# Key-value sums of a linear-attention and MLP kernel: two groups of eight token tiles in the place of three groups of six, six and four

## The chip, the cores and the metric

The kernel runs on one core of one Trainium2 chip. The core has five engines that work side by side, each through an instruction list of its own: PE (TensorE, matrix products), DVE (VectorE), ACT (ScalarE), POOL (GpSimd) and SP (SyncE, which here only issues DMAs). They meet through semaphores: an instruction waits until another engine's counter has reached a value, and everything behind it on its own engine waits with it. The metric is the time of one execution on the device, in microseconds; lower is better.

## The reference, cut to what matters

The input is one sequence of 2048 tokens with 448 features, in bf16. After a layernorm, two branches are computed and added to it.

```python
xn = layernorm(x)                                  # x: (1, 2048, 448)
# branch A: 16 heads of 28, linear attention with a softmax feature map
q, k, v = split(xn @ wqkv)                         # per head
phi(t)  = concat(softmax(t @ w_phi), softmax(-t @ w_phi))
kv  = einsum("bhsf,bhsd->bhfd", phi(k), v)         # sum over all 2048 tokens
z   = phi(k).sum(over tokens)
num = phi(q) @ kv;  den = phi(q) @ z + 1e-6
A   = (num / den) @ wo
# branch B: a token-shifting MLP
h   = gelu(layernorm(xn) @ w1);  hs = shift(h) @ w2;  x1 = xn + hs
B   = x1 + gelu(layernorm(x1) @ w3) @ w4           # w3: 448 x 1792, w4: 1792 x 448
out = xn + A + B
```

The change is about `kv` (and `z`, which is computed with it): a sum over all tokens that must be complete before the first `num` can be computed.

## The kernel before, in words

The 2048 tokens are 16 tiles of 128, and four tiles make a token group of 512. One token tile is one block of 128 partitions. All data stays in SBUF; PSUM has eight banks, and each is reused many times.

A recorder (`Recorder`, lines 19 to 222) takes every operation in the order in which the Python code calls it, works out from the bytes that each one reads and writes which waits are needed, and then plays each engine's list. So an engine's order is the order of the calls that use it, and moving a call in the list moves its instructions only against those of the same engine. Because helpers record everything, all matrix products have line 204 in the profile, activations line 212, other element-wise work line 216.

After a first stage (layernorm, v, the w1 products and the start of the feature maps) the order is written out by hand in one list, lines 1055 to 1079, of pairs of a short name and its arguments. The names that matter here:

- `k0(n)`, `k1(n)`, `q0(n)`, `q1(n)`: the two halves of the phi products of token tiles 2n and 2n+1. `k1` and `q1` end with two exponentials on ACT. `kn(n)` (DVE) and `kx(n)` (POOL) normalise phi(k) afterwards.
- `w0(i)`, `w1_(i)`: the two halves of the w2 product of tiles i and i+1; `w1_` ends with two additions on DVE, which read PSUM banks 4 and 5 for i = 12 and 14.
- `K(i)` = `kv_tile`, the key-value sum of token tile i: 16 matrix products of 128 rows by 30 columns over 64 columns, all added up in PSUM bank 6. It reads `vaug` (v, a column of ones) and `phik` (phi(k)).
- `kc` = `kv_turn` and `kb` = `kv_blocks`, one DVE instruction each: the finished sum is transposed out of bank 6, then spread into `kvq`, which the attention products read.
- `a(p)`, `b(p)`: the two halves of w3 pair p, that is of 256 of the 1792 columns for 512 tokens. Pairs 0 to 6 belong to the first token group, 7 to 13 to the second. `a` is 8 products, `b` is 6, and `b` ends with one gelu on ACT that reads two PSUM banks into `h3T`. Even pairs use banks 2 and 3, odd pairs banks 0 and 1, so `a(p)` may start only when the gelu of pair p-2 has read its banks.
- `N(i)` = `num_tile` and `o_T`: the attention of token tile i. 16 products go to banks 6 and 7; DVE reads them with a reciprocal, three multiplications or additions and one more combined operation, then inverts the denominator; POOL divides, a DMA transposes. Every `N` uses the same two banks, so the next one waits for the last of these reads.
- `f(n, k)`: quarter n of the output products of tiles 2k and 2k+1; `f(1, k)` and `f(2, k)` are 28 products each and use w4.
- `AD(i)`, `A(i)`: the second layernorm's application on DVE or POOL; `G(i)`, `T(i)`, `S(i)` are DMAs; `lo(i)` is a layernorm statistic on DVE.

Two functions in the code:

```python
741        def kv_tile(i):
742            for n in range(4):
743                for j in range(4):
744                    h = 8 * (j // 2) + 2 * n + j % 2
745                    R.mm(banks[6][HP * j:HP * j + VP, 64 * n:64 * n + 64], vaug[:, i, VP * h:VP * h + VP],
746                         phik[:, i, 2 * h:2 * h + 2, :].rearrange("p g e -> p (g e)"), i == 0 and n == 0, False)

807            b = 1 - p % 2
808            a = lap_pair([banks[2 * b + k] for k in range(2)],
...
812            def late():
813                a[1]()
814                R.act(h3T[:, g % 2, fc:fc + 2, :], two(2 * b), ACT.Gelu_apprx_tanh)
```

Nearly all other products use the array as two halves of 64 rows, two products at a time, one in each half; `K` uses all 128 rows, with four column strips. Buffers are shared: `h3T` lies over `phik` (pair p overwrites the bytes of token tile p, for p up to 13), and the scratch of `N` and of the output lies over `vaug`. Tile i of the key-value sum must therefore be done before the gelu of pair i writes.

Before, PE's order in the part that is changed is: the end of `q0(7)`; K of tiles 0, 7, 8, 3, 1, 5; `q1(7)`, `w1_(12)`; K of tiles 2, 4, 9, 10, 11, 6; a0 a1 b0 b1; `w0(14)`; a2 a3 b2 b3; `w1_(14)`; a4 a5 b4 b5; K of tiles 15, 14, 13, 12; a6 a7 b6 b7; N1, f(1,0), N0; a9 a8 b9 b8; N3, f(2,0), N2; and so on. DVE has `kc` and `kb` behind `AD(11)`, then the work of N1, `AD(10)`, `AD(9)`, the work of N0, `lo(12)`, the work of N3, `lo(15)`, the work of N2.

Of the kernel before, what the change touches and what calls it, by code (L numbers as in the profile page):

```python
# [224 lines left out]
def bass_parallel_sum__linear_kernel_hedgehog__mixer_s_mlp__prompt_kernel(  # L225
# [17 lines left out]
    with es:  # L243
# [807 lines left out]
        def wo_in(eng="SP"):  # L1051
            load_lap(wo, A_wo, (eng, eng))

        K, G, S, T, kc, kb, W = kv_tile, g_T, store, q_T, kv_turn, kv_blocks, fin_tails
# [4 lines left out]
            (kn, 3), (T, 2), (kx, 3), (w1_, 6), (lo, 2), (lo, 3), (q1, 4), (k0, 5), (sc, 0), (k0, 6), (k1, 5),  # L1059
            (w0, 8), (k1, 6), (kn, 4), (w1_, 8), (A, 0), (T, 5), (q0, 5), (q0, 6), (T, 4), (q1, 5), (AD, 1), (w0, 10),  # L1060
            (T, 7), (A, 3), (k0, 7), (kn, 5), (A, 2), (w1_, 10), (q1, 6), (lo, 7), (w0, 12), (k1, 7), (lo, 4),
            (q0, 7), (lo, 5), (T, 6), (load_w4, 1), (lo, 6), (K, 0), (kx, 4), (K, 7), (K, 8), (K, 3), (kn, 6), (K, 1),
            (G, 0), (G, 1), (K, 5), (q1, 7), (w1_, 12), (kx, 5), (K, 2), (K, 4), (G, 3), (kn, 7), (K, 9), (G, 2),
            (K, 10), (lo, 11), (sc, 4), (A, 7), (lo, 10), (A, 6), (AD, 5), (K, 11), (K, 6), (a, 0), (a, 1), (A, 4),
            (b, 0), (lo, 8), (b, 1), (load_w4, 0, g_tok[:, 3, :]), (lo, 9), (kx, 6), (w0, 14), (kx, 7), (a, 2), (G, 6), (a, 3),
            (b, 2), (sc, 8), (b, 3), (w1_, 14), (a, 4), (a, 5), (b, 4), (G, 7), (G, 5), (b, 5), (G, 4), (lo, 13),
            (K, 15), (K, 14), (K, 13), (K, 12), (T, 12), (AD, 11), (T, 11), (T, 8), (kc,), (kb,), (a, 6), (T, 9),
            (a, 7), (b, 6), (b, 7), (N, 1), (AD, 10), (AD, 9), (G, 10), (f, 1, 0), (N, 0), (a, 9), (a, 8), (G, 9),
            (b, 9), (lo, 12), (b, 8), (N, 3), (lo, 15), (f, 2, 0), (N, 2), (a, 10), (AD, 8), (a, 11), (G, 11),
            (b, 10), (f, 3, 0), (lo, 14), (sc, 12), (b, 11), (G, 8), (f, 4, 0), (AD, 14), (a, 12), (T, 14), (a, 13),  # L1070
            (S, 1), (N, 5), (f, 1, 1), (b, 13), (f, 3, 1), (AD, 15), (T, 10), (N, 4), (b, 12), (T, 13), (T, 15),
# [42 lines left out]
```

## Time and profile before

| what | value |
|---|---|
| three runs | 170.65, 170.97 and 173.65 us, median 170.97 |
| the profiled execution's own time | 171.18 us |
| its span in the profile | 169.4 us |
| busy: PE, DVE, POOL, ACT | 164.9, 109.3, 88.0, 81.9 us |
| granted TensorE clock | 1.00 of full speed |

The span runs from the first instruction's start to the last one's end; 1.8 us of the execution's own time lie outside it. Matrix products overlap, so busy PE says that products are under way and not that PE works at its peak: what counts is from when to when a group of products is started. In a timeline each row has the start, the time from the first start to the last end, engine, line, operation, what is written and read, the shape, and how many instructions were merged; in brackets stands the idle time before it and what ended that. The next row's start tells how long PE really spent on a row. In such rows `K` reads `phik,vaug`, w3 pairs read `gT,w`, `N` reads `kvq`, w2 reads `hT` and `hRT`, and `f(1, k)` and `f(2, k)` read `w,phik`.

### The profile page before, as it was taken

How to read it: one execution, taken by the hardware profiler on the slowest of the kernel's cores; microseconds unless marked ns; L12 is line 12 of the kernel's file. 1: busy time of each engine (PE TensorE's matmuls, PEld its weight loads, DVE VectorE, ACT ScalarE, POOL GpSimd, SP SyncE). 2: the span in 40 equal slices, each digit the busy share in tenths (PEclk: the TensorE clock that was granted, in tenths of full speed). 3: DMA queues.
4: the chain of work that ended last, by engine and by line, in shares of the span. 5: the costliest groups of instructions: out<-in, count | busy, mean ns of one | idle time of the engine just before them, and what ended most of it. 6: DMA issues, size and time to landing. Idle time of an engine off the chain costs nothing.

```text
span 169.4 us, 5409 instructions
## 1 busy us (share of the span) xinstructions
PE 164.9 (97%) x2355; PEld 101.2 (60%) x2355; DVE 109.3 (64%) x248; ACT 81.9 (48%) x112; POOL 88.0 (52%) x119
## 2 busy tenths in 40 slices
PE   8799999999999999999999999999999999999994
PEld 7467778776888875535554555554555555544453
DVE  3689854459999999973998766833753647340031
ACT  4589976769998877455242240424310404024000
POOL 5378990002999999890455274362263342734040
PEclk9999999999999999999999999999999999999999
DMA  5995455599999670959464575753412112113011
GB/s 155 353 209 96 77 95 148 115 275 251 272 164 167 199 96 5 223 115 138 92 67 92 65 151 100 151 122 91 86 40 60 58 31 60 33 31 112 0 54 54
DMA packets 50583, 19.93 MB, mean 118 GB/s; under 512 B 41728, under 2 KB 49856, under 8 KB 50560
## 3 DMA queue, kind: packets, MB, share of 16 engines
q1 hardware_dynamic: 49440, 18.71, 56.1%
q10 hardware_dynamic: 1120, 0.89, 1.7%
q8 instruction: 18, 0.29, 0.8%
q14 instruction: 5, 0.04, 0.1%
HBM read 7.14 MB, written 1.84 MB: 53 GB/s over the span
## 4 chain that ended last, share of the span: by engine, by line
PE 92%; DMA 3%; DVE 2%; POOL 1%; SPq 0%; issue 0%
PE banks L204 91%; DMA xtok<-in_A_x_dram 3%; DVE st L216 1%; PE banks L208 1%; POOL rs L216 1%; SPq L222 0%; DVE mv L216 0%; POOL xn L216 0%; DVE xn L216 0%; DVE vaug L216 0%
## 5 line engine op out<-in xcount | busy, mean ns | idle before, releaser
L212 ACT ACTIVATE phik<-banks 128x1024 bf16<-128x1024 f32 (+1 forms) x44 | 41.2, 988 | 62.4 <-PE banks L204 62.3
L216 DVE TENSOR_TENSOR vaug<-banks,vaug 128x464 f32<-128x464 f32 (+3 forms) x65 | 32.8, 514 | 21.4 <-PE banks L204 19.7
L204 PE MATMUL banks<-gT,w 64*128 64x512 bf16 x392 | 46.5, 376 | 0.1
L204 PE MATMUL banks<-w,phik 64*128 64x448 bf16 (+3 forms) x434 | 45.2, 343 | 0.0
L216 POOL TENSOR_TENSOR xnT<-vaug 128x280 bf16<-128x280 f32 (+1 forms) x32 | 18.2, 589 | 41.9 <-DVE vaug L216 41.9
L739 POOL TENSOR_TENSOR phik<-phik,rks 128x1792 bf16<-128x1792 bf16 x8 | 25.6, 3212 | 17.4 <-DVE rks L216 16.9
L204 PEld LDWEIGHTS banks<-w,phik 64*128 64x128 bf16 (+1 forms) x434 | 22.5, 94 | 19.3 <-issue 0.4
L204 PE MATMUL banks<-wv,xnT 64*128 64x448 bf16 (+2 forms) x222 | 32.2, 346 | 0.0
L204 PEld LDWEIGHTS banks<-gT,w 64*128 64x128 bf16 x392 | 18.5, 94 | 20.1 <-ACT phik L212 1.5
L216 POOL TENSOR_TENSOR vaug<-xn,xtok 128x448 f32<-128x448 bf16 x16 | 16.2, 1031 | 8.8 <-DVE vaug L216 8.8
L204 PEld LDWEIGHTS banks<-wv,xnT 64*128 64x128 bf16 (+1 forms) x222 | 13.9, 94 | 7.9 <-PE banks L204 0.5
L204 PE MATMUL banks<-xnT,w 64*128 64x512 bf16 (+1 forms) x105 | 16.7, 334 | 0.0
L216 DVE TENSOR_REDUCE ksum<-phik 128x64 f32<-128x1792 bf16 x8 | 16.0, 1997 | 0.2 <-ACT phik L212 0.2
L216 DVE RECIPROCAL vaug<-banks 128x16 f32<-128x16 f32 x16 | 4.0, 252 | 18.7 <-PE banks L204 18.7
L204 PE MATMUL banks<-wpk,xnT 64*128 64x448 bf16 x112 | 15.7, 349 | 0.0
L204 PE MATMUL banks<-wpq,xnT 64*128 64x448 bf16 x112 | 15.2, 349 | 0.0
L212 ACT ACTIVATE hi<-banks 128x896 bf16<-128x896 f32 x16 | 14.0, 936 | 2.1 <-PE banks L204 2.1
L204 PE MATMUL banks<-w,hT 64*128 64x448 bf16 x96 | 14.4, 349 | 0.0
L216 POOL TENSOR_TENSOR rs<-mv,mhalf 128x1 f32<-128x1 f32 (+1 forms) x14 | 9.7, 700 | 1.9 <-DVE mv L216 1.9
L204 PEld LDWEIGHTS banks<-wpk,xnT 64*128 64x128 bf16 x112 | 9.2, 94 | 2.0
L216 DVE TENSOR_TENSOR xn<-banks,xn 128x512 bf16<-128x512 f32 (+1 forms) x16 | 8.9, 596 | 2.0 <-PE banks L204 2.0
L216 DVE BATCH_NORM_STATS2 st<-xtok 128x6 f32<-128x448 bf16 x15 | 9.1, 604 | 1.5 <-DMA xtok<-in_A_x_dram 1.5
(68 smaller groups left out, 167.6 us busy)
## 6 DMA issues: line engine op xcount, KB each, us to landing
w<-in_B_w_dram SPq DMA_DIRECT2D x2, 896.0 KB, 5.7
out_dram<-vaug SPq DMA_DIRECT2D x15, 112.0 KB, 1.9
w<-in_B_w_dram SPq DMA_DIRECT2D x2, 784.0 KB, 5.3
xtok<-in_A_x_dram SPq DMA_DIRECT2D x2, 448.0 KB, 6.8
wv<-in_A_wo_dram SPq DMA_DIRECT2D x2, 224.0 KB, 4.1
xtok<-in_A_x_dram SPq DMA_DIRECT2D x3, 112.0 KB, 4.4
xtok<-in_A_x_dram ACTq DMA_DIRECT2D x3, 112.0 KB, 4.6
w<-in_B_w_dram SPq DMA_DIRECT2D x1, 336.0 KB, 3.9
```

The lines of the kernel that those rows point to most:

```text
L204: self.op("PE", lambda e: e.matmul(out, lhsT, rhs, start=start, stop=stop, skip_group_check=True), [out], [lhsT, rhs], tile=self._tile(lhsT))
L208: self.op("PE", lambda e: e.transpose(out, in_, ident), [out], [in_, ident], tile=self._tile(in_))
L212: self.op("ACT", lambda e: e.activation(out, in_, func, **kw), [out], [in_] + aps)
L216: self.op(eng, lambda e: getattr(e, name)(out, *args, **kw), [out], aps)
L739: R.op(pool, lambda e: e.tensor_tensor(ph, ph, wide, op=ALU.mult), [ph], [ph, wide, *after])
```

## The change

Only the order in the list changes. The K of tiles 0 to 7 now stand together, behind `q1(7)` and `w1_(12)`. The K of tiles 8 to 15 stand together, behind a6 a7 b6 b7 (pair 7 is the first of the second token group), followed by `kc` and `kb`. The halves a9 and a8 are moved from behind N0 to ahead of N1.

```diff
-            (q0, 7), (lo, 5), (T, 6), (load_w4, 1), (lo, 6), (K, 0), (kx, 4), (K, 7), (K, 8), (K, 3), (kn, 6), (K, 1),
-            (G, 0), (G, 1), (K, 5), (q1, 7), (w1_, 12), (kx, 5), (K, 2), (K, 4), (G, 3), (kn, 7), (K, 9), (G, 2),
-            (K, 10), (lo, 11), (sc, 4), (A, 7), (lo, 10), (A, 6), (AD, 5), (K, 11), (K, 6), (a, 0), (a, 1), (A, 4),
+            (q0, 7), (lo, 5), (T, 6), (load_w4, 1), (lo, 6), (kx, 4), (kn, 6), (G, 0), (G, 1), (q1, 7), (w1_, 12), (K, 0), (K, 7),
+            (K, 3), (K, 1), (K, 5), (K, 2), (K, 4), (K, 6), (kx, 5), (G, 3), (kn, 7), (G, 2), (lo, 11), (sc, 4), (A, 7),
+            (lo, 10), (A, 6), (AD, 5), (a, 0), (a, 1), (A, 4),
             (b, 0), (lo, 8), (b, 1), (load_w4, 0, g_tok[:, 3, :]), (lo, 9), (kx, 6), (w0, 14), (kx, 7), (a, 2), (G, 6), (a, 3),
             (b, 2), (sc, 8), (b, 3), (w1_, 14), (a, 4), (a, 5), (b, 4), (G, 7), (G, 5), (b, 5), (G, 4), (lo, 13),
-            (K, 15), (K, 14), (K, 13), (K, 12), (T, 12), (AD, 11), (T, 11), (T, 8), (kc,), (kb,), (a, 6), (T, 9),
-            (a, 7), (b, 6), (b, 7), (N, 1), (AD, 10), (AD, 9), (G, 10), (f, 1, 0), (N, 0), (a, 9), (a, 8), (G, 9),
+            (T, 12), (AD, 11), (T, 11), (T, 8), (a, 6), (T, 9),
+            (a, 7), (b, 6), (b, 7), (K, 8), (K, 9), (K, 10), (K, 11), (K, 13), (K, 12), (K, 15), (K, 14), (kc,), (kb,),
+            (a, 9), (a, 8), (N, 1), (AD, 10), (AD, 9), (G, 10), (f, 1, 0), (N, 0), (G, 9),
             (b, 9), (lo, 12), (b, 8), (N, 3), (lo, 15), (f, 2, 0), (N, 2), (a, 10), (AD, 8), (a, 11), (G, 11),
```

The number of instructions and the data that each reads and writes are the same. On every engine other than PE the order of the instructions stays as it was.

## Prediction

> **What bounds the kernel now.** First the page: busy times, and the chain of work that ended last.
>
> ```profile
> span 169.4 us, 5409 instructions
> PE 164.9 (97%) x2355; PEld 101.2 (60%) x2355; DVE 109.3 (64%) x248; ACT 81.9 (48%) x112; POOL 88.0 (52%) x119
> PE 92%; DMA 3%; DVE 2%; POOL 1%; SPq 0%; issue 0%
> ```
>
> PE is busy for 97% of the span and holds 92% of the chain. So time is won only where PE issues sooner, and lost wherever PE must wait. Next the waits of PE's weight loads from 40 us on, which come ahead of each product and so show what PE waits for (total, times, longest):
>
> ```profile
> PEld banks L204 <- ACT phik L212: 1.9, 8, 0.4
> ```
>
> In 130 us the largest entry is 1.9 us, and much of that is hidden behind products still running. There is almost no idle PE to remove; the question is whether the new order keeps PE as full. Now PE's timeline through the changed part.
>
> ```profile
> 61.48 0.98 PE L204 MATMUL banks<-wpq,xnT 64*128 64x448 bf16 x8
> 62.39 1.08 PE L204 MATMUL banks<-phik,vaug 128*30 128x64 bf16 x96
> 63.41 0.74 PE L204 MATMUL banks<-wpq,xnT 64*128 64x448 bf16 x6
> 63.98 0.73 PE L204 MATMUL banks<-w,hT 64*128 64x448 bf16 x6
> 64.64 0.95 PE L204 MATMUL banks<-phik,vaug 128*30 128x64 bf16 x96
> 65.70 3.20 PE L204 MATMUL banks<-gT,w 64*128 64x512 bf16 x28
> 68.72 0.75 PE L204 MATMUL banks<-w,hT 64*128 64x448 bf16 x6
> ...
> 72.50 0.75 PE L204 MATMUL banks<-w,hT 64*128 64x448 bf16 x6
> 73.15 3.25 PE L204 MATMUL banks<-gT,w 64*128 64x512 bf16 x28
> 76.32 0.77 PE L204 MATMUL banks<-phik,vaug 128*30 128x64 bf16 x64
> ...
> 77.03 3.20 PE L204 MATMUL banks<-gT,w 64*128 64x512 bf16 x28
> 80.06 0.38 PE L204 MATMUL banks<-kvq,eqT_lo 64*128 64x60 bf16 x16
> 80.28 2.81 PE L204 MATMUL banks<-w,phik 64*128 64x448 bf16 x28
> 82.93 0.38 PE L204 MATMUL banks<-kvq,eqT_lo 64*128 64x60 bf16 x16
> 83.15 3.18 PE L204 MATMUL banks<-gT,w 64*128 64x512 bf16 x28
> 86.17 0.38 PE L204 MATMUL banks<-kvq,eqT_lo 64*128 64x60 bf16 x16
> 86.39 2.81 PE L204 MATMUL banks<-w,phik 64*128 64x448 bf16 x28
> 89.04 0.38 PE L204 MATMUL banks<-kvq,eqT_lo 64*128 64x60 bf16 x16
> ```
>
> Start to next start gives PE's prices. 28 w3 products take 68.72 - 65.70 = 3.02 us, 0.216 per concurrent pair: 0.86 for an `a`, 0.65 for a `b`. f(1,0) takes 82.93 - 80.28 = 2.65, 0.189 per pair; an N 0.22. A K group of 64 products takes 77.03 - 76.32 = 0.71, of 96 takes 63.41 - 62.39 = 1.02: 9.7 ns per product and about 0.09 beside. Entering: the six products at 63.98 would be followed at 64.55, and K starts at 64.64, 0.09 late (0.15 at 62.39).
>
> Then the two engines that PE may have to wait for: ACT's gelus and the last of its exponentials, and DVE.
>
> ```profile
> 72.07 1.94 ACT L212 ACTIVATE phik<-banks 128x1024 bf16<-128x1024 f32 x2 [1.84 <-PE banks L204]
> 75.79 1.94 ACT L212 ACTIVATE phik<-banks 128x1024 bf16<-128x1024 f32 x2 [1.78 <-PE banks L204]
> 79.62 1.94 ACT L212 ACTIVATE phik<-banks 128x1024 bf16<-128x1024 f32 x2 [1.89 <-PE banks L204]
> ...
> 91.84 1.02 ACT L212 ACTIVATE phik<-banks 128x1024 bf16<-128x1024 f32 x1 [4.17 <-PE banks L204]
> ```
>
> ```profile
> 66.61 1.09 DVE L216 TENSOR_TENSOR xn<-banks,xn 128x512 bf16<-128x512 f32 x2
> ...
> 77.17 0.45 DVE L216 STREAM_TRANSPOSE w<-banks 128x256 f32<-128x256 f32 x1 [0.21 <-PE banks L204]
> 77.66 0.65 DVE L216 TENSOR_TENSOR kvq<-w,pick 128x464 bf16<-128x464 f32 x1
> 80.49 0.26 DVE L216 RECIPROCAL vaug<-banks 128x16 f32<-128x16 f32 x1 [2.18 <-PE banks L204]
> ...
> 82.34 0.18 DVE L216 SCALAR_TENSOR_TENSOR vaug<-banks,vaug 128x16 f32<-128x16 f32 x1
> ...
> 82.72 0.98 DVE L216 TENSOR_SCALAR g_tok<-xn,mv,rs 128x512 bf16<-128x512 bf16 x2
> 83.63 0.24 DVE L216 RECIPROCAL vaug<-banks 128x16 f32<-128x16 f32 x1
> ...
> 85.47 0.18 DVE L216 SCALAR_TENSOR_TENSOR vaug<-banks,vaug 128x16 f32<-128x16 f32 x1
> ...
> 88.45 0.18 DVE L216 SCALAR_TENSOR_TENSOR vaug<-banks,vaug 128x16 f32<-128x16 f32 x1
> ```
>
> **The change, step by step**, in the clock of this trace. No instruction is added or removed; what changes is which work covers which wait.
>
> *1. First group, a gain that is mostly a loan.* q0(7) is done issuing at 61.48 + 4 x 0.19 = 62.24. q1(7) and w1_(12) now follow at once, 64.55 - 63.41 = 1.14 us. With 0.09 to enter, K starts at 63.47. Eight tiles are 128 products; the second group of before, 96 products up to a0, took 65.70 - 64.64 = 1.06 (a0 has several waits to pass), so 1.06 + 32 x 0.0097 = 1.37 and a0 starts at 64.84, 0.86 earlier. Of this, four tiles' worth (64 products, 0.62) comes back in the second group. The rest, 0.24, is the gap of one group fewer. Bounds for what a group costs in gaps: nothing, if the neighbours' starts hide it, and 0.15 + 0.13 = 0.28 with the widest entry and a0's slower exit (1.06 - 96 x 0.0097); I take the 0.24 that the rows add up to. Up to b5 all of PE then runs 0.86 earlier. Cover: w0(14) would start at 67.86 and needs the additions of w1_(12) out of banks 4 and 5, which end on DVE at 66.61 + 1.09 = 67.70: 0.16 us of slack, so no wait, and not much more could be gained here.
>
> [...]
>
> *2. A new wait ahead of a6.* In before, the four K tiles stand between b5 and a6. Now a6 follows b5. a6 writes banks 2 and 3, which the gelu of pair 4 must have read. In before that gelu runs from 75.79 for 1.02 and b5's last slot ends at 76.32 - 0.09 = 76.23. Shifted by 0.86: PE is free at 75.37, the gelu ends at 75.95. A semaphore takes about 0.05 us. The row at 72.07 shows the same wait at its edge: that gelu ends at 73.09 and a4 starts at 73.15, although w1_(14), the row at 72.50, lies between. So a6 starts at 76.00: **0.63 us of wait**. Behind it on PE stand a7, b6, b7 and the K group; ACT waits for b6. a7 needs the second gelu of that row, done at 75.79 + 1.94 - 0.86 = 76.87, and starts at 76.92, 0.06 late.
>
> *3. K8 to K15, then a9, a8, N1.* a7 from 76.92, b6 77.78, b7 78.43, its last slot ends at 79.08. K enters at 79.17; 128 products by the rows are 0.71 + 64 x 0.0097 = 1.33, so PE is free at 80.50. a9 needs the gelu of pair 7. In before b6 ends at 77.03 + 2 x 0.86 + 0.65 = 79.40 and its gelu starts at 79.62, 0.22 later; now it starts at 78.65, and the two end 1.94 later at 80.59. a9 starts at 80.64 (**0.14 wait**), a8 at 81.50, N1 at 82.36. The sum itself is no bound: the last K starts at 80.41; in before from there (77.03 - 0.09 = 76.94) to the end of `kb` (77.66 + 0.65 = 78.31) is 1.37, so `kvq` is ready at 81.78, with a9 and a8 as its cover. Without that cover N1 would lose 1.3 us. N1 comes 2.30 later than its 80.06, with 1.72 of a9 and a8 already done: a net loss of 0.58.
>
> *4. The work that covered N0's reads is gone.* Between N0 and N3 stood a9, a8, b9, b8 (3.02 us); now only b9 and b8 (1.30). N3 writes banks 6 and 7, so it waits for DVE's last read for N0, the combined operation at 85.47, done at 85.65, which is 5.59 us behind N1's start at 80.06. That DVE stretch is full (the reads for N1 end at 82.52, the denominator, then AD(10) and AD(9) for 0.98, the reads for N0 from 83.63 without idle time), its order is unchanged, and it starts with N1. So N3 can start 5.64 after N1, at 88.00. PE would be there after 0.22 + 2.65 + 0.22 + 1.30 = 4.39, at 86.75: **1.25 us of wait**, the largest term. f(2,0) and N2 stand behind it, and DVE's work for N3. The same once more for N2: the reads for N3 end at 88.63, 8.57 behind N1, hence N2 at 82.36 + 8.62 = 90.98, while PE is ready at 88.00 + 2.87 = 90.87: 0.11 more. From N2 on PE has the order of before; N2 was at 89.04, so all comes **1.94 us later**.
>
> Sum: a6 0.63, a7 0.06, a9 0.14, N3 1.25, N2 0.11 are 2.19; less 0.24 is 1.95, which closes with N2's own 1.94. Against the profiled execution (span 169.4, own time 171.18) that makes 173.1; it lies 0.2 above the median of the runs, 170.97, from which I forecast 170.97 + 1.94 = **172.9 us**. The measurement can tell about 2% from no change (3.4 us), so this counts as no change, on the slow side.
>
> **Rivals.**
>
> *No net wait* (the new gaps fall on cover, only the saved group counts): 170.97 - 0.24 = 170.7. It needs gelus that end 0.6 us sooner and DVE 1.25 us ahead. For it speaks that ACT idles before each pair of gelus (1.8 us); against it, that this idle time ends with PE, so ACT can't start sooner. 10%.
>
> *Only the front counts*: the N3 wait is absorbed because DVE, idle for 2.18 us ahead of N1, has more in hand than I see. Then 0.58 remains: 171.5. Against: `AD(10)` and `AD(9)` stand behind N1's work in DVE's list. 12%.
>
> *The granted clock falls* in the longer wait. Point: if 1.25 us of idle PE near N3 lowers the clock to half for the next f(2,0), that costs its 2.65 us again: 170.97 + 1.94 + 2.65 = 175.6, clearly slower. This row has PE idle for 1.08 of 4 us at the start (the third number from its end is the granted clock):
>
> ```profile
> 4.00:8.00 4.00, 2.92 (x61) 1.70 (x57) 2.32 (x7) 2.48 (x8) 1.33 (x2) 1.00 1.08 351
> ```
>
> The clock there is 1.00, so I give this 6%. [...]
>
> **How the numbers follow.** Forecast 72%, by its bounds 172.2 to 173.6: 0.2 below for the group's upper bound, some 0.5 either way for what the runs differ among themselves. The range 171.0 to 173.8 takes in that case and the second rival, and leaves out the first and the third with a rest for small waits that I have not seen. Over 2% faster (below 167.6) none of the cases gives: 2%. Over 2% slower (above 174.4): the clock, and a rest, 8%. Within: 90%.
>
> **What would show it.** In the changed trace: two K groups of 128 products; a0 about 0.9 us earlier; PE idle ahead of a6, released by ACT, 0.6 us; a short one ahead of a9; N1 at about 82.4; N3 about 5.6 us behind N1, with over 1 us idle released by DVE; from N2 on the same rows 1.9 us later. I would be wrong if DVE ran the reads for N0 sooner behind N1, if something else held N1, for example the transposed queries, or if f(3,0) now waited for the attention of N0.

## The result, and the profile after

The changed kernel is slower by 1.4%: the ratio to the kernel before is 1.0142, 95% interval 1.0114 to 1.0170, that is 2.4 us on 171.0 (1.9 to 2.9). Three of its six executions took 173.24 to 173.72 us; the other three fell into a slower state and took 176.49 to 176.59, which lifts the plain median to 175.11, outside the forecast range, and the ratio leaves such executions out on both sides.

The page after:

```profile
span 171.6 us, 5409 instructions
PE 165.3 (96%) x2355; PEld 101.2 (59%) x2355; DVE 109.2 (64%) x248; ACT 81.7 (48%) x112; POOL 88.1 (51%) x119
PEclk9999999999999999999999999999999999999999
PE 90%; DVE 4%; ACT 3%; DMA 1%; issue 1%; DVEq 0%; ACTq 0%
```

The work is the same (PE's busy time differs by 0.4 us), the span is 2.2 us longer, and DVE and ACT now hold 7% of the chain that ended last. The row `PEclk` gives the granted clock in 40 equal slices of the span: 9 is 90% of full speed or more. PE's timeline through the changed part; brackets give idle time and what ended it:

```profile
60.81 1.78 PE L204 MATMUL banks<-wpq,xnT 64*128 64x448 bf16 x14
62.43 0.73 PE L204 MATMUL banks<-w,hT 64*128 64x448 bf16 x6
63.09 1.22 PE L204 MATMUL banks<-phik,vaug 128*30 128x64 bf16 x128
64.41 3.20 PE L204 MATMUL banks<-gT,w 64*128 64x512 bf16 x28
...
71.86 3.25 PE L204 MATMUL banks<-gT,w 64*128 64x512 bf16 x28
75.58 1.04 PE L204 MATMUL banks<-gT,w 64*128 64x512 bf16 x8 [0.47 <-ACT phik L212]
77.16 2.33 PE L204 MATMUL banks<-gT,w 64*128 64x512 bf16 x20 [0.54 <-issue]
79.43 1.36 PE L204 MATMUL banks<-phik,vaug 128*30 128x64 bf16 x128
80.88 1.90 PE L204 MATMUL banks<-gT,w 64*128 64x512 bf16 x16
82.62 0.38 PE L204 MATMUL banks<-kvq,eqT_lo 64*128 64x60 bf16 x16
...
85.49 0.38 PE L204 MATMUL banks<-kvq,eqT_lo 64*128 64x60 bf16 x16
...
88.26 0.39 PE L204 MATMUL banks<-kvq,eqT_lo 64*128 64x60 bf16 x16 [1.09 <-DVE vaug L216]
...
91.16 0.39 PE L204 MATMUL banks<-kvq,eqT_lo 64*128 64x60 bf16 x16
```

This execution reached q0(7) at 60.81, before at 61.48, so it runs 0.67 us ahead for reasons older than the change. N2 is at 91.16 against 89.04: with the head start, 2.79 us were lost on the way. Of these, 2.79 - 0.67 = 2.12 us are left in this execution's own time, 173.30 us against the 171.18 of the profiled execution before.

Idle time in brackets counts from the modelled end of a product. The loss is measured from the start that was due. The 28 products from a4 to b5 took 0.06 more than 14 x 0.216 us before (from 73.15 to 76.23). So they are issued by 71.86 + 14 x 0.216 + 0.06 = 74.94, and a6 starts at 75.58, 0.64 late.

### The profile page after: what moved, and what is told of

Same layout as the page of the kernel before. It is cut to its first block, busy times and chain, and to the rows that moved or that the text cites. A ratio compares the mean times of both kernels' runs of the same rounds, so it can differ in the third digit from the quotient of the medians.

```text
span 171.6 us, 5409 instructions
## 1 busy us (share of the span) xinstructions
PE 165.3 (96%) x2355; PEld 101.2 (59%) x2355; DVE 109.2 (64%) x248; ACT 81.7 (48%) x112; POOL 88.1 (51%) x119
## 4 chain that ended last, share of the span: by engine, by line
PE 90%; DVE 4%; ACT 3%; DMA 1%; issue 1%; DVEq 0%; ACTq 0%
PE banks L204 88%; DVE vaug L216 3%; ACT phik L212 2%; DMA xtok<-in_A_x_dram 1%; PE banks L208 1%; DVE g_tok L216 1%; ACT xn L482 0%; DVE st L216 0%; ACT xnT L212 0%; ACT rs L212 0%; DVE mv L216 0%; DVEq L166 0%; ACTq L166 0%
## 5 line engine op out<-in xcount | busy, mean ns | idle before, releaser
L204 PEld LDWEIGHTS banks<-wpq,xnT 64*128 64x128 bf16 x112 | 8.5, 94 | 2.7 <-PE banks L204 0.5
```

What stands on the lines that cost most here:

```text
L204: self.op("PE", lambda e: e.matmul(out, lhsT, rhs, start=start, stop=stop, skip_group_check=True), [out], [lhsT, rhs], tile=self._tile(lhsT))
```

## The experiments

My theory: the grouping is nearly free, and the loss is the sum of separate waits of PE that the old order covered, ahead of a6 (ACT), a7, a9, and N3 (DVE). The rivals: the groups of 128 are slow themselves, or the order behind them does not matter because later work absorbs a wait. Ratios are to the kernel before, with 95% intervals. These are 0.2 to 0.6% wide to either side, so pieces of half a microsecond (0.3%) are read from the traces, each of one execution, between landmarks that both traces have.

**The grouping alone** (e1_front).

```diff
 # against the changed kernel
-(a, 7), (b, 6), (b, 7), (K, 8) .. (K, 14), (kc,), (kb,), (a, 9), (a, 8), (N, 1), ..., (N, 0), (G, 9),
+(K, 8) .. (K, 14), (T, 12), (AD, 11), (T, 11), (T, 8), (kc,), (kb,), (a, 6), (T, 9), (a, 7), (b, 6), (b, 7),
+(N, 1), ..., (N, 0), (a, 9), (a, 8), (G, 9),
```

> Only the grouping is changed: K0 to K7 together behind q1(7) and w1_(12), K8 to K15 together at the old place of the third group, between b5 and a6; kc, kb, a9 and a8 stand where they stood before. Theory of the waits (the changed kernel loses by a6, a7 and N3 waiting, not by the groups): one group's gap less, 0.24 us, against 0.22 us that q1(7) lost directly behind q0(7) in the changed kernel's trace, so 171.0 us, within 0.3 of before; PE shows no wait over 0.1 us ahead of a6, a7, a9 or N3. Rival (groups of 128 products are slow themselves, or the early w3 pairs hurt something): at least 1 us slower than before, 172 us or more.

Measured: 1.0029 (1.0007 to 1.0050), 0.5 us slower. Its PE timeline:

```profile
60.87 1.79 PE L204 MATMUL banks<-wpq,xnT 64*128 64x448 bf16 x14
...
63.16 1.22 PE L204 MATMUL banks<-phik,vaug 128*30 128x64 bf16 x128
...
75.12 1.57 PE L204 MATMUL banks<-phik,vaug 128*30 128x64 bf16 x128
76.62 3.19 PE L204 MATMUL banks<-gT,w 64*128 64x512 bf16 x28
79.65 0.38 PE L204 MATMUL banks<-kvq,eqT_lo 64*128 64x60 bf16 x16
```

No bracket stands ahead of a6 or N1: with its old followers, the group of eight makes nothing wait. From q0(7) to N1 it takes 18.78 us, before 80.06 - 61.48 = 18.58. So the grouping by itself gains nothing, and the rival that blames it for the whole loss (1 us or more) fails. There are two reasons why it is no gain. q0(7) and q1(7) now follow each other: their 14 products take 62.43 - 60.81 = 1.62 us in the changed kernel where 7 x 0.189 is 1.32. From 40 us on, the waits of PE's weight loads in that kernel hold an entry that the kernel before does not have there, 0.5 us for PE's own products:

```profile
PEld banks L204 <- PE banks L204: 0.5, 1, 0.5
```

It is the load for the first product of q1(7), at 61.85. Both halves write the same two banks, with the halves of the array exchanged (lines 555 to 560), so the second has the first one's products to wait for. And the second group takes 76.62 - 75.12 = 1.50 us, 0.17 more than the 1.33 that I worked out; more on this below.

**The swap that undoes the first** (e6_front_swap).

```diff
 # against e1_front
-(q1, 7), (w1_, 12), (K, 0), (K, 7),
+(w1_, 12), (q1, 7), (K, 0), (K, 7),
```

> The kernel with only the grouping changed (two groups of eight, the second between b5 and a6, kc, kb, a9, a8 where they were before), and in addition w1_(12) ahead of q1(7) so that the two halves of the same phi product do not follow each other. Theory: the wait of 0.22 us between q0(7) and q1(7) is gone, while q1(7)'s exponentials end 0.3 to 0.6 us later and still before a1 needs its banks; 0.2 us faster than without the swap, 171.0 us, ratio 1.001 to before, 0.998 at best. Rival (the later exponentials hold a1): as without the swap, 171.3 us, with a wait ahead of a1.

Measured: 0.9996 (0.9973 to 1.0018). That is 0.3% below e1_front, as expected in sign, but the intervals overlap. The trace of e10_844, a variant below with the same swap, shows it more sharply:

```profile
60.94 0.98 PE L204 MATMUL banks<-wpq,xnT 64*128 64x448 bf16 x8
...
62.99 1.22 PE L204 MATMUL banks<-phik,vaug 128*30 128x64 bf16 x128
```

From q0(7) to the first K it takes 62.99 - 60.94 = 2.05 us, in e1_front 63.16 - 60.87 = 2.29: the swap gives back 0.24 us, so the two halves do cost time when they follow each other.

**The back part alone** (e2_back).

```diff
 # against the kernel before; its first two groups stay
-(K, 15), (K, 14), (K, 13), (K, 12), (T, 12), (AD, 11), (T, 11), (T, 8), (kc,), (kb,), (a, 6), (T, 9), (a, 7), (b, 6), (b, 7), (N, 1),
+(T, 12), (AD, 11), (T, 11), (T, 8), (a, 6), (T, 9), (a, 7), (b, 6), (b, 7), (K, 15), (K, 14), (K, 13), (K, 12), (kc,), (kb,), (a, 9), (a, 8), (N, 1),
-(N, 0), (a, 9), (a, 8), (G, 9),
+(N, 0), (G, 9),
```

> Only the back part is changed: the first two groups of six stay as before, and the last group (tiles 15, 14, 13, 12) stands behind b7, with a9 and a8 ahead of N1. Theory of the waits: a6 waits about 0.64 us for a gelu, a7 0 to 0.7 for the transposed second token group, a9 about 0.5 (the group is half as long, 0.62 less cover), N3 1.1 to 1.25 us, N2 up to 0.1: 2.4 to 3.2 us in all, so 173.4 to 174.2 us. Rival (the grouping costs it): within 0.5 us of before, 171.5 or less.

Measured: 1.0169 (1.0138 to 1.0199), 2.9 us. Its PE timeline:

```profile
76.89 3.25 PE L204 MATMUL banks<-gT,w 64*128 64x512 bf16 x28 [0.47 <-ACT phik L212]
80.07 0.69 PE L204 MATMUL banks<-phik,vaug 128*30 128x64 bf16 x64
81.53 1.90 PE L204 MATMUL banks<-gT,w 64*128 64x512 bf16 x16 [0.77 <-ACT phik L212]
...
88.90 0.40 PE L204 MATMUL banks<-kvq,eqT_lo 64*128 64x60 bf16 x16 [1.09 <-DVE vaug L216]
```

The whole loss is there with the old grouping: from q0(7), at 61.49 in this trace, to N2 at 91.81 it takes 30.32 us, 2.76 more than before. a6 waits as in the changed kernel (0.47), N3 too (1.09). a9 waits more (0.77), because a group of 64 covers less of pair 7's gelu than one of 128. a7 does not wait here: the 28 products from a6 on run through.

**What holds N3** (e3_ad_early, e5_a9_back, e9_a8_back).

```diff
 # e3_ad_early, against the changed kernel
-(K, 15), (K, 14), (kc,), (kb,), ..., (N, 1), (AD, 10), (AD, 9), (G, 10),
+(K, 15), (K, 14), (AD, 10), (AD, 9), (kc,), (kb,), ..., (N, 1), (G, 10),
 # e5_a9_back, against the changed kernel
-(kc,), (kb,), (a, 9), (a, 8), (N, 1), ..., (N, 0), (G, 9),
+(kc,), (kb,), (N, 1), ..., (N, 0), (a, 9), (a, 8), (G, 9),
 # e9_a8_back, against the changed kernel
-(kc,), (kb,), (a, 9), (a, 8), (N, 1), ..., (N, 0), (G, 9),
+(kc,), (kb,), (a, 9), (N, 1), ..., (N, 0), (a, 8), (G, 9),
```

> The changed kernel with the two applications AD(10) and AD(9) moved on DVE from behind N1's work to ahead of kc, into DVE's idle time before the key-value sum is done. Theory of the waits: they take 0.98 us out of the DVE stretch that N3 waits for, so N3 starts about 4.75 us behind N1 and waits some 0.3 us in place of 1.25; 0.9 us faster than the changed kernel, 172.4 us (ratio to before 1.008). Rival (N3's wait is not what costs the time, since later work would absorb it): like the changed kernel, 173.3 us.

Measured: 1.0155 (1.0121 to 1.0189), no faster than the changed kernel, as the rival had it; the expectation of 1.008 was wrong. The trace shows why. DVE in this run:

```profile
83.36 0.26 DVE L216 RECIPROCAL vaug<-banks 128x16 f32<-128x16 f32 x1 [0.88 <-PE banks L204]
...
86.23 0.26 DVE L216 RECIPROCAL vaug<-banks 128x16 f32<-128x16 f32 x1 [0.56 <-PE banks L204]
...
88.08 0.18 DVE L216 SCALAR_TENSOR_TENSOR vaug<-banks,vaug 128x16 f32<-128x16 f32 x1
```

Without the two applications DVE sits idle for 0.56 us and then waits for N0 itself, which PE can't deliver before f(1,0) is done. N0's reads start 86.23 - 83.36 = 2.87 behind N1's, the very distance of N0 from N1 on PE, where before it was 83.63 - 80.49 = 3.14. Only that 0.27 of the 0.98 was in the way, too little for the timed ratio to tell. N2 follows N1 by 91.22 - 82.94 = 8.28 us in the place of 8.54, so up to there nothing absorbs what N3 gains; the applications were merely not what the wait hung on. The rest of N3's wait is the reads of N0 themselves, 88.26 - 86.23 = 2.03 us, against 1.30 us of b9 and b8.

> The changed kernel with a9 and a8 back behind N0, where they stood before; all else as changed. Theory (N3 waits because a9 and a8 no longer cover N0's reads on DVE): N3's wait of 1.25 us is gone, but N1 now stands directly behind the key-value sum and waits for its transpose and spreading, some 1.3 us; the net is within 0.3 us of the changed kernel, 173.1 us, with the idle time moved from N3 to N1. Rival (N3's wait comes from something else): it stays, N1's wait is added, 174.5 us.

Measured: 1.0160 (1.0130 to 1.0190). PE:

```profile
76.72 1.04 PE L204 MATMUL banks<-gT,w 64*128 64x512 bf16 x8 [0.47 <-ACT phik L212]
...
83.30 0.40 PE L204 MATMUL banks<-kvq,eqT_lo 64*128 64x60 bf16 x16 [1.44 <-DVE kvq L216]
...
89.42 0.38 PE L204 MATMUL banks<-kvq,eqT_lo 64*128 64x60 bf16 x16
...
92.28 0.38 PE L204 MATMUL banks<-kvq,eqT_lo 64*128 64x60 bf16 x16
```

With a9 and a8 back in their place, N3 (89.42) has no bracket: its wait was missing cover. The idle time has moved to N1, which waits 1.44 us for `kvq`. From a6 to N2 it takes 15.56 us, in the changed kernel 91.16 - 75.58 = 15.58: the same 1.72 us of products can cover one of the two waits.

> The changed kernel with only a8 moved back behind N0; a9 stays ahead of N1. Theory (what counts is how many products lie between N0 and N3, and between the key-value sum and N1): N1 waits 0.3 us for the spread sum, N3 0.4 in place of 1.25, so 0.55 us faster than the changed kernel, 172.7 us, ratio 1.011. Rival (N3's wait does not depend on a8): N3 waits 1.25 and N1 0.3, 173.6 us.

Measured: 1.0130 (1.0102 to 1.0157); in the trace 15.03 us from a6 to N2, 0.55 less than in the changed kernel:

```profile
75.65 1.04 PE L204 MATMUL banks<-gT,w 64*128 64x512 bf16 x8 [0.47 <-ACT phik L212]
77.05 2.33 PE L204 MATMUL banks<-gT,w 64*128 64x512 bf16 x20 [0.36 <-DMA gT<-g_tok]
...
82.12 0.39 PE L204 MATMUL banks<-kvq,eqT_lo 64*128 64x60 bf16 x16 [0.31 <-DVE kvq L216]
...
87.77 0.40 PE L204 MATMUL banks<-kvq,eqT_lo 64*128 64x60 bf16 x16 [0.23 <-DVE vaug L216]
...
90.68 0.39 PE L204 MATMUL banks<-kvq,eqT_lo 64*128 64x60 bf16 x16
```

That is the expected amount, but partly by luck: a7 follows a6 by 1.40 us here and by 1.58 in the changed kernel, so 0.18 of it lies ahead of a7 and only 0.37 behind. With one half of a pair on either side, N1 and N3 wait 0.31 and 0.23 in the place of 1.09 at N3 alone. The rival (N3 does not depend on a8) is out. The timed ratio moves the right way but less than the two intervals can tell.

**What holds a7** (e7_g4_first).

```diff
 # against the changed kernel
-(G, 7), (G, 5), (b, 5), (G, 4),
+(G, 7), (G, 4), (b, 5), (G, 5),
```

> The changed kernel with the DMA transposes G(4) and G(5) swapped on SP: G(4), whose data is ready by 68 us, is issued right behind G(7) and not last behind G(5). In the changed kernel's trace a7 started 0.67 us after the gelu that it needs, released with the landing of G(4), which took 4.5 us from its issue. Theory (a7 waits for that landing): G(4) lands before 75 us, and unless G(5), now last, lands as late, a7 follows the gelu; 0.6 us faster than the changed kernel, 172.7 us. Rival one (whichever transpose is last before T(12) takes 4.5 us): G(5) is late in its place, a7 waits as before, 173.3 us. Rival two (the landing was chance in that execution): no change, 173.3 us, and a7's wait differs between profiles.

Measured: 1.0127 (1.0097 to 1.0157). PE:

```profile
76.02 3.25 PE L204 MATMUL banks<-gT,w 64*128 64x512 bf16 x28 [0.47 <-ACT phik L212]
79.19 1.22 PE L204 MATMUL banks<-phik,vaug 128*30 128x64 bf16 x128
80.65 1.90 PE L204 MATMUL banks<-gT,w 64*128 64x512 bf16 x16 [0.24 <-ACT phik L212]
...
90.93 0.39 PE L204 MATMUL banks<-kvq,eqT_lo 64*128 64x60 bf16 x16
```

a6 to b7 runs in one piece, so a7 did wait for the landing of G(4). Three other traces name that wait: in e3_ad_early, e5_a9_back and e9_a8_back a7 is idle for 0.44, 0.50 and 0.36 us until the DMA that writes `gT`. In the changed kernel G(4) was issued at 72.6 and landed 4.5 us later, at 77.1, where a7 starts at 77.16. a9 now has idle time (0.24), since less time is left for its gelu. From a6 to N2 it takes 14.91 us, 0.67 less than in the changed kernel. The timed ratio moves the right way, but less than the two intervals can tell. In the changed kernel the DMA engines nearly stopped while G(4) and the next transpose were under way:

```profile
73.50:74.75 1.25, 1.25 (x16) 0.52 (x12) 1.05 (x3) 0.25 (x1) 1.25 (x2) 1.00 1.74 111
74.75:76.25 1.50, 1.03 (x12) 0.31 (x8) 0.37 (x1) 1.50 (x2) 1.00 (x2) 1.00 0.05 6
```

The last two numbers are the DMA share and GB/s: 111, then 6. What pauses them is not settled. In e2_back a7 has no such wait: there G(4) landed at most 2.7 us after its issue. One thing stands out in the traces: in the changed kernel, e3_ad_early, e5_a9_back and e9_a8_back a packet of the instruction queue (in the changed kernel between 74.0 and 74.2) comes 0.4 to 0.8 us ahead of the pause, and before and e2_back have neither the packet nor a pause of that length there. Not every such packet is followed by a pause, and no run tests the link.

**The price of a group** (e4_seven_groups).

```diff
 # against the kernel before: tiles of the first two groups, two at a time
+(q0, 7) K0 K7 (q1, 7) K8 K3 (w1_, 12) K1 K5 ... (a, 0) K2 K4 (a, 1) K6 K9 (b, 0) K10 K11 (b, 1)
```

> The kernel before with its key-value sums in seven groups in the place of three, tiles and order of the rest unchanged: two tiles behind q0(7), two behind q1(7), two behind w1_(12), two behind a0, two behind a1, two behind b0, and the last four between b5 and a6 as before. Theory: a group costs 0.21 us in gaps (0.09 to enter, 0.12 to leave), so four more cost 0.8 us: 171.6 us, ratio 1.005, and the profile shows 0.28 and 0.13 us at each new entry and exit. Rival (a change of the array's mode is hidden by neighbouring work): no change, 170.8 us. [...]

Measured: 1.0023 (1.0004 to 1.0041), 0.4 us for four more groups. PE:

```profile
61.38 0.98 PE L204 MATMUL banks<-wpq,xnT 64*128 64x448 bf16 x8
62.30 0.42 PE L204 MATMUL banks<-phik,vaug 128*30 128x64 bf16 x32
...
69.32 0.73 PE L204 MATMUL banks<-w,hT 64*128 64x448 bf16 x6
```

From q0(7) to w0(14) it takes 7.94 us, before 68.72 - 61.48 = 7.24: 0.70 for four groups, 0.18 each. That is a little below the 0.21 expected here and the prediction's 0.24; the timed 0.4 (0.1 to 0.7) is half of the 0.8 expected. "No cost" is just outside the interval.

**A candidate and a repair** (e10_844, e11_repaired).

```diff
 # e10_844, against the kernel before
+(q0, 7), ..., (w1_, 12), (q1, 7), K0 K7 K3 K1 K5 K2 K4 K6, ..., (w1_, 14), K8 K9 K10 K11, (a, 4), (a, 5), (b, 4), (b, 5), K13 K12 K15 K14, ..., (a, 6)
 # e11_repaired, against the changed kernel: e7_g4_first, e9_a8_back and the swap of e6_front_swap together
```

> A candidate to beat both: K0 to K7 together behind w1_(12) and q1(7) in this order, K8 to K11 between w1_(14) and a4, K12 to K15 between b5 and a6; the rest as before the change. Theory (time is only won where PE's own waits go): against before the three groups remain, a4's small wait for a gelu (0.06 us) is covered, and no group of 128 products stands late where one stalled inside itself by up to 0.4 us in the profile of the swapped variant; 170.6 us, ratio 0.997 to 1.000. Rival (the groups' places do not matter once all waits are covered): 1.000, and I would not be able to tell them apart.

> The changed kernel with three repairs at once: G(4) ahead of G(5), a8 back behind N0, w1_(12) ahead of q1(7); the second group still stands behind b7. Theory (the losses are separate waits and add up): a6 0.64, a7 0.04, a9 0.1, N1 0.3, N3 0.25 us remain, against 0.21 for the group saved: 1.1 us over before, ratio 1.006 to 1.008. Rival (one wait grows by what another loses, as with a7 and a9): 1.011 or more.

Measured: e10_844 0.9982 (0.9940 to 1.0024), not to be told from no change; its trace takes 18.37 us from q0(7) (60.94) to N1 (79.31), 0.21 less than before. e11_repaired 1.0113 (1.0057 to 1.0169), a wide interval that holds the expected 1.006 to 1.008 and the rival's 1.011 alike. Its trace takes 14.33 us from a6 to N2, 1.25 less than the changed kernel, where e7_g4_first and e9_a8_back gained 0.67 and 0.55 one by one. Up to the K group the gain is 0.67, as in e7_g4_first; behind it 0.58, where e9_a8_back alone gained 0.37. So in the traces the repairs do not eat each other up; that the two sums agree to 0.03 us is partly chance, and the timed ratio does not decide.

**Inside a group** (e12_long).

```diff
 # against e6_front_swap; the sum of tiles 8 to 15 is taken three times
-(b, 5), ..., (K, 8) .. (K, 14), (T, 12)
+(b, 5), ..., (K, 8) .. (K, 14), (K, 8) .. (K, 14), (K, 8) .. (K, 14), (T, 12)
```

> A look at what stalls inside a K group: the variant with two groups and the swap, in which the sums of tiles 8 to 15 are added three times over (so the key-value sum is not the reference's), 384 products in a row in the place of 128. Theory (PE's instructions come in blocks of 16 KB, the 18 packets of the instruction queue, and a group of such short products uses one up faster than the next arrives): after the first one or two hundred products the group stalls repeatedly, mean 11 to 13 ns per product, 4.2 to 5 us in all. Rival (the stalls come with something else at that place, a DMA or POOL): one stall, the rest at 8.06 ns, 3.2 to 3.5 us in all.

Measured: 180.28 us in one execution. PE, four stretches (busy PE, PEld, DVE, ACT and POOL, then the granted clock, the DMA share and GB/s), and the instruction queue:

```profile
74.95 2.76 PE L204 MATMUL banks<-phik,vaug 128*30 128x64 bf16 x248
80.55 1.43 PE L204 MATMUL banks<-phik,vaug 128*30 128x64 bf16 x128 [2.85 <-issue]
84.00 0.29 PE L204 MATMUL banks<-phik,vaug 128*30 128x64 bf16 x8 [2.02 <-issue]
84.23 5.09 PE L204 MATMUL banks<-gT,w 64*128 64x512 bf16 x28
89.17 0.38 PE L204 MATMUL banks<-kvq,eqT_lo 64*128 64x60 bf16 x16
```

```profile
80.60:82.00 1.40, 1.38 (x128) 1.23 (x128) 0.00 (x0) 0.00 (x0) 0.00 (x0) 0.75 1.03 231
82.10:84.00 1.90, 0.00 (x0) 0.00 (x0) 0.00 (x0) 0.00 (x0) 0.00 (x0) 0.50 0.00 0
84.30:88.10 3.80, 3.80 (x20) 1.30 (x22) 1.10 (x2) 0.00 (x0) 0.00 (x0) 0.50 0.02 4
88.40:92.00 3.60, 3.60 (x54) 1.83 (x50) 2.24 (x7) 1.94 (x2) 0.01 (x1) 1.00 0.00 0
```

```profile
q8 instruction: 20, 0.33, 0.8%
```

The 384 products take 84.23 - 74.95 = 9.28 us, worse than either expectation. They come as 248, 128 and 8, with idle stretches of 2.85 and 2.02 us in which PE waits for nothing the profile shows. 128 products are 256 instructions with their weight loads. Against the 18 packets of the instruction queue in the kernel before and after there are 20 here, for 512 instructions more: 256 instructions per packet, just what the 128 products between the two stalls hold. In the trace one packet of that queue moves between 77.6 and 77.8 and one between 81.6 and 81.8, at the start of either stall or just ahead of it, and PE goes on 2.2 to 3.0 us behind each. During the second stall no other engine works and the DMA engines move nothing, so the rival (a DMA or POOL at that place) has nothing to point to. All this fits a PE that ran out of instructions, but the arrival of an instruction at PE is not in the trace, so that is my reading of it. It would fit the smaller stalls inside late groups of 128 too (the 0.17 us of e1_front); for those it is argued, not shown.

## Why the prediction was right

The verdict (no change by the 2% bound, on the slow side), the sign and the mechanism held: 1.94 us forecast, 2.4 (1.9 to 2.9) measured. But the trace lost 2.79 us between q0(7) and N2, and two terms that make up the difference were not foreseen. That the number stayed within the range is owed to the range's width, not to them. By its steps:

*Step 1, half right.* a0 came 65.70 - 64.41 - 0.67 = 0.62 us earlier, not 0.86. The saved group was there, but I had priced the join of q0(7) and q1(7) at nothing: their 14 products took 0.3 us longer, of which the swap gave back 0.24. The trace of before has no place where two halves of one phi product follow each other in this part, and I did not bound it. The 0.2 us that the forecast's lower bound takes off for a group's upper bound no run shows: the rows' 0.28 would be 0.04 beyond the 0.24, and in e4_seven_groups a group cost 0.18.

*Step 2, a6 right, a7 mis-sized.* a6 waited 0.64 us, forecast 0.63; e2_back and e7_g4_first show the same 0.47 of idle time, and with the group back in its place (e1_front) it is gone. a7 started 77.16 - 75.58 = 1.58 us behind a6, 0.72 more than its 0.86, where I had 0.06. The prediction has no term for the landing of the second token group's transposes; e7_g4_first shows that a7 hung on one of them.

*Step 3, right.* a9 lost about 0.1 us (0.14 forecast), and `kvq` was ready ahead of N1 as long as both a9 and a8 stood between; e5_a9_back priced the cover at 1.44 us of idle time, against my 1.3.

*Step 4, right in size, its reason partly wrong.* N3 started 88.26 - 82.62 = 5.64 us behind N1, as forecast, with 1.09 us of idle time released by DVE. That the two agree to the hundredth is luck. I called that DVE stretch full. e3_ad_early shows that 0.27 of it could be taken away and no more, because N0's place behind f(1,0) is the next bound. N2 followed 8.54 behind N1 (8.62 forecast).

The sum of what was missed: 0.66 at a7, about 0.24 at q1(7), less 0.08 at N2, is 0.82; 1.94 and 0.82 make 2.76, against 2.79 in the trace.

Of the rivals, "no net wait" fell with the brackets at a6 and N3, and "only the front counts" with the one at N3. So did the rival of the falling clock: the clock stayed at 1.00 through the wait ahead of N3 (87.2 to 88.2 us) and through f(2,0) behind it (to 91.2). e12_long shows one case in which it does fall. Behind the idle stretch of 2.85 us it was 0.75 on average while PE was at work again (80.60 to 82.00), and 0.50 through the second stretch of 2.02 us and up to 88.10. The next 28 w3 products took 89.17 - 84.23 = 4.94 us for the usual 3.02, and from 88.40 on the clock was 1.00 again. So 1.09 us of idle time came without a fall (1.44 us too: the profiled execution of e5_a9_back has a mean clock of 1.00) and 2.85 us with one behind it; where between them it begins no run here shows.

## What to carry to other kernels

When one engine is 97% busy, a block of work is worth what it covers: before moving it, list which wait ends just behind its old place, and look for a cover of the same length there. Moving the same 1.7 us of products from one wait to another only chose which wait shows. In the traces, splitting them (e9_a8_back) was about 0.4 us better from a7 to N2 than either place, too little for the timed ratios to tell. A DMA whose landing something longer has always covered belongs on that list too, by its landing and not by its issue.

## What the runs showed of the hardware that I had not expected

In e12_long 248 products of 64 columns went out in 2.76 us, then PE stood still for 2.85 us, and behind the next 128 for 2.02 us. My reading, from the packets of the instruction queue at either stall, is that such short products outran the instruction supply. In e10_844, whose groups behind w3 products hold 64, no such stall shows (64 products took 0.62 us between b5 and a6); that shorter groups save time is not shown, since its ratio cannot be told from 1. And four more groups, each with two changes of the array between halves of 64 rows and the whole of 128 rows, cost 0.70 us from q0(7) to w0(14), 0.18 each (e4_seven_groups).
